# Hourglass attention and quick-GELU MLP: the schedule of batch 0 regrouped over ScalarE, GpSimd and TensorE

## Chip, cores and metric

The kernel runs on one core of a Trainium2 chip. The time is device microseconds of one execution: the median of 3 runs before the change is 320.51 us (320.23, 320.51 and 321.03).

## The reference

Two stages. Stage 1 is attention over q, k, v of 8 batches, 8 heads, 576 positions, head size 64, and is the sum of two parts: a coarse one, on q, k and v averaged over four neighbours (144 positions), repeated four times, and a local one with a band mask of width 3.

```python
q_d = q.reshape(B, H, Sd, factor, D).mean(axis=3)      # factor 4; k_d, v_d alike
out_up = np.repeat(sm_attn(q_d, k_d, v_d), factor, axis=2)
mask = np.abs(pos[:, None] - pos[None, :]) < factor
scores = np.where(mask, scale * np.matmul(q, k.transpose(0, 1, 3, 2)), -1e9)
out_local = np.matmul(softmax(scores), v)
x = (out_up + out_local).transpose(0, 2, 1, 3).reshape(B * S, H * D)
```

Stage 2 is an MLP on the 4608 rows of x (512 wide, hidden 2048):

```python
h = x @ w_in
out = (h * (1.0 / (1.0 + np.exp(-1.702 * h)))) @ w_out
```

## The kernel before, in words

The MLP runs over nine groups of 512 rows. While TensorE works through the MLP of group g, the attention of batch g+1 is woven into it at fixed places (lists POS and POS_0, numbers of MLP steps). Only batch 0 has no MLP beside it: its attention stands in the open at the head of the program, and the change is made there. All engines follow an order written out by hand (a manual schedule): each engine runs its instructions in program order, and waits only for what an instruction needs.

Matrices in PSUM are PA[0], PA[1], PA[2] (two banks each) and PM[0], PM[1] (one bank each). Heads go in four pairs, hp = 0 to 3. For each pair batch 0 does the following:

- **Transposes** (L262, VectorE): k and q of four heads (a quad, qd = 0 or 1) are brought into kT and qT.
- **Sums over four** for the coarse part: `reduce_qk` on VectorE (L281) or `pool_qk` on GpSimd (L292, L296) make kdT and qdT.
- **Scores** on TensorE: local (L360, after a constant bar from L348), coarse (L372). **exp** on ScalarE: L410 and L416.
- **v sums**: `prep_vd_pe`, matmuls with the selection matrix psel (L329) and a copy by ScalarE (L338). psel itself is made of four ramps: GpSimd iotas of 192 and 256 columns (L99, L101), then Abs, Relu and Exp on ScalarE (L170 to L173).
- **AV**: `av_local0` (L519) and `av_down0` (L533, L542) into o[hp], which is PA[0], PA[1], PA[2] and PA[0] again for hp = 0, 1, 2, 3.
- **Normalising**: `normalise0` on VectorE (reciprocal L561, products L564 into yd and L569 into yl), for pairs 0 to 2 in parts "a" and "b".
- **Transposing and summing**: `turned` issues `transp_sum` (L584, L595) on TensorE, and `copy_x` (L607, L611), by which ScalarE writes xT[hp].
- **First MLP product of group 0**: `part`, matmuls of xT[dmc] with w_in (L712), as soon as xT of that pair is there; then Silu on ScalarE (L723), and the second product with w_out (L776).

Ahead of the first `turned` TensorE runs two fp32 matmuls on zeros (`warm(2, t=PM[0], z=wf)`, L657; each appears as two passes), and ScalarE loads the Silu table (L859) and copies the mask (L134). `warm` elsewhere is filler work on bf16 zeros.

GpSimd issues nearly all early loads, in this order: k, q of batch 0 (4 loads), v of batch 0 (10, L216), w_in (4 chunks of 512 columns, L238), k, q of batch 1 (4, L185), w_out 0 and 1 (L247), v of batch 1 chunks 0 to 2 (6 loads), then the GpSimd sums of batch 1, then v chunks 3 and 4 (4 loads), w_out 2 and 3. In the compiled program these loads use eight semaphores in turn: load number n waits on GpSimd until load n-8 has landed. The sums of batch 1's first quad (L292, L296) stand behind the sixth v load of batch 1, which waits for q of batch 1's second quad.

The second product of group 0 has 64 matmuls (numbers 0 to 63): w_out chunk 0 for rows 0 to 255 is used by numbers 0 to 7, chunk 1 by 8 to 15, both for the other rows by 16 to 31, chunk 2 from number 32, chunk 3 from 48. Scores of batch 1 come ahead of number 0 and of number 14, its v sums ahead of number 25, its first AV ahead of number 30.

Of the kernel before, what the change touches and what calls it, by code (L numbers as in the profile page):

```python
# [19 lines left out]
def kernel(  # L20
# [70 lines left out]
    dr = consts.tile([128, 1], FP32, name="dr")  # L91
    bias = consts.tile([128, 4], FP32, name="bias")
    dp = consts.tile([128, 7, 64], FP32, name="dp")
    it = dict(allow_small_or_imprecise_dtypes=True)
    halves = [slice(0, 64), slice(64, 128)]

    def iota_psel():
        for par in range(2):
            nc.gpsimd.iota(dp[halves[par], 0:3], pattern=[[-72, 3], [-8, 64]],  # L99
                           base=2 * (KSTART[par] + 72) - 3, channel_multiplier=2, **it)  # L100
            nc.gpsimd.iota(dp[halves[par], 3:7], pattern=[[72, 2], [-384, 2], [-8, 64]],  # L101
                           base=2 * (KSTART[par] + 114) - 3, channel_multiplier=2, **it)

    def iota_mask():
        for par in range(2):
# [61 lines left out]
        nc.vector.tensor_tensor(out=rv, in0=rv, in1=r2, op=ALU.add)  # L167

    def end_psel():
        nc.scalar.activation(out=dp, in_=dp, func=AF.Abs)  # L170
        nc.scalar.activation(out=dp, in_=dp, func=AF.Relu, bias=bias[:, 3:4])
        for sl, c in ((slice(0, 1), 1), (slice(1, 7), 0)):
            nc.scalar.activation(  # L173
                out=psel[:, sl], in_=dp[:, sl],
                func=AF.Exp, scale=-400.0, bias=bias[:, c : c + 1],
            )
# [17 lines left out]
    def load_qk(b, qd):  # L194
        load_1("k", k, kf, b, qd)
        load_1("q", q, qf, b, qd)
# [40 lines left out]
    def load_w_in(c, n):  # L237
        nc.gpsimd.dma_start(  # L238
            out=w_in_bf[:, :, c : c + n],
            in_=bass.AP(  # L240
                tensor=moe_w_in.tensor, offset=moe_w_in.offset + c,
                ap=[[d_ff, 128], [128 * d_ff, n_dmc], [1, n]],
            ),
        )
# [187 lines left out]
    def banks(t):  # L432
        return t if t is PM else [t[:, u, :] for u in range(2)]

    def av_local(b, hp, o, chunks=range(5)):
        E, vb, o = es[hp], vbs[b % 2], banks(o)
        for i in chunks:
            for par in range(2):
                for j in range(2):
                    pos = j if par == 0 else 1 - j  # L440
                    nc.tensor.matmul(  # L441
                        o[par][64 * pos : 64 * pos + 64, 65 * i : 65 * i + 65],
                        lhsT=E[64 * par : 64 * par + 64, j, 60 * i : 60 * i + 64],
                        rhs=vb[64 * par : 64 * par + 64, i, 2 * hp + j, :],
                        start=True, stop=True,
                        tile_position=(64 * par, 64 * pos),
                    )
# [63 lines left out]
        return x  # L511

    def av_local0(hp, o, chunks):
        E, vb = es[hp], vbs[0]
        for i in chunks:
            for j in range(2):
                for par in range(2):
                    pos, c0 = i % 2, 65 * (i // 2 * 2 + j)
                    nc.tensor.matmul(  # L519
                        o[64 * pos : 64 * pos + 64, par, c0 : c0 + 65],  # L520
                        lhsT=E[64 * par : 64 * par + 64, j, 60 * i : 60 * i + 64],
                        rhs=vb[64 * par : 64 * par + 64, i, 2 * hp + j, :],
                        start=True, stop=True,
                        tile_position=(64 * par, 64 * pos),
                    )

    def av_down0(hp, o):
        Ed, vd, u = eds[hp // 2], vds[0], hp % 2
        h0 = hp - u
        for kc in range(3):  # L530
            for j in range(2):
                q0 = SD * kc + 128
                nc.tensor.matmul(  # L533
                    o[64:128, j, 260:390],
                    lhsT=Ed[64 * j : 64 * j + 48, u, q0 : q0 + 64],
                    rhs=vd[64 * j : 64 * j + 48, kc, h0 : h0 + 2, :],
                    start=(kc == 0), stop=(kc == 2),
                    tile_position=(64 * j, 64),
                )
        for kc in range(3):  # L540
            for j in range(2):
                nc.tensor.matmul(  # L542
                    o[:, j, 390:455],
                    lhsT=Ed[64 * j : 64 * j + 48, u, SD * kc : SD * kc + 128],
                    rhs=vd[64 * j : 64 * j + 48, kc, hp, :],
                    start=(kc == 0), stop=(kc == 2),
                    tile_position=(64 * j, 0),
                )
# [5 lines left out]
            work.tile([128, 2, 7, 1], FP32, name="rc0", tag="rc0", bufs=4),  # L554
        )

    def normalise0(o, y, u, parts="ab"):
        yl, yd, rc = y
        ov = o[:, :, 0:455].rearrange("p x (c e) -> p x c e", e=65)
        c0, c1 = {"a": (0, 4), "b": (4, 7), "ab": (0, 7)}[parts]  # L560
        nc.vector.reciprocal(rc[:, :, c0:c1], ov[:, :, c0:c1, 64:65])  # L561
        if "b" in parts:
            st = 2 - u
            nc.vector.tensor_tensor(  # L564
                out=yd.rearrange("p s x d -> p x s d"), in0=ov[:, :, 4 + u : 7 : st, 0:D],
                in1=rc[:, :, 4 + u : 7 : st].to_broadcast([128, 2, 2, D]), op=ALU.mult,
            )
            c1 = 6
        nc.vector.tensor_tensor(  # L569
            out=yl[:, :, c0:c1], in0=ov[:, :, c0:c1, 0:D],  # L570
            in1=rc[:, :, c0:c1].to_broadcast([128, 2, c1 - c0, D]), op=ALU.mult,
        )
# [247 lines left out]
    fill()  # L820
    for i in range(5):
        load_vb(0, i)
    for c in range(4):
        load_w_in(512 * c, 512)
    for qd in range(NQ):
        load_qk(1, qd)
    load_w_out(0)
    load_w_out(1)
    warm(21, 336)
    make_off()  # L830
    make_ident(di)
# [8 lines left out]
    prep_1("k", 0, 1)  # L840
    prep_1("q", 0, 1)
    reduce_qk(0, 0, "q")
    reduce_qk(0, 1, "k")
    reduce_qk(0, 1, "q")
    warm(10)
    sp = scores(0, 1, PA[0:2])
    exp_local(1, sp)
    exp_down(0, scores_d(0, 0, PA[2]))
    warm(4)
    for hp in range(4):  # L850
        o[hp] = PA[hp % 3]
        y[hp] = y_tiles0()
    prep_vd_pe(0, PM[0], range(0, 2))
    for hp in range(2):
        av_local0(hp, o[hp], range(5))
        normalise0(o[hp], y[hp], hp % 2, "a")
    prep_vd_pe(0, PM[1], range(2, 3))
    exp_down(1, scores_d(0, 1, PA[2]))
    nc.scalar.preload_act_table_set("silu_and_others")  # L859
    for hp in range(2):  # L860
        av_down0(hp, o[hp])
        normalise0(o[hp], y[hp], hp % 2, "b")
    av_local0(2, o[2], range(5))
    normalise0(o[2], y[2], 0, "a")
    warm(2, t=PM[0], z=wf)
    make_mask()

    gT0 = new_gT()
    acc = PM + [PA[n][:, u, :] for n in (1, 2, 0) for u in range(2)]
    late = [acc[n] for n in (0, 1, 6, 2, 4, 0, 1, 7, 0, 1)]  # L870

    def part(ffcs, *dmcs):
        for dmc in dmcs:
# [5 lines left out]
        transp_sum(y[hp], x)  # L879
        copy_x(0, hp, PM if n is None else PA[n][:, :, 0:288])  # L880

    turned(0, None)
    av_down0(2, o[2])
    normalise0(o[2], y[2], 0, "b")
    turned(1, 1)
    av_local0(3, o[3], range(5))
    av_down0(3, o[3])
    normalise0(o[3], y[3], 1)
    part((0, 1), 0)
    turned(2, 2)  # L890
    part((0, 1), 1)
    part((2, 3), 0)
    turned(3, 0)
    part((2, 3), 1)
    part((0, 1, 2, 3), 2)
    part((4, 5), 0, 1, 2)
    part(range(6), 3)
# [4 lines left out]
    for g in range(n_groups):  # L902
        b = g + 1
        if g == 0:
            load_vb(1, 0)
            load_vb(1, 1)
            load_vb(1, 2)
            prep_qk(1, 0)
            pool_qk(1, 0)
            prep_qk(1, 1)  # L910
            load_vb(1, 3)
            load_vb(1, 4)
            load_w_out(2)
            load_w_out(3)
            reduce_qk(1, 1, "q")
            reduce_qk(1, 1, "k")
            for qd in range(NQ):
                load_qk(2, qd)
            nc.gpsimd.memset(v4[32:64], 0.0)
            load_v(2, gate=after(w_out_bf[0:1, 12, 0:1], nc.gpsimd))  # L920
            load_v4(2)
        elif b < B:
            if b > 2:
                load_v4(b)
            prep_qk(b, 0)
            pool_qk(b, 0)
            if b + 1 < B:
                for qd in range(NQ):
                    load_qk(b + 1, qd)
            prep_v(b, nc.gpsimd)  # L930
            if b + 1 < B:
                load_v(b + 1)
            prep_qk(b, 1)
            pool_qk(b, 1)
            prep_v4(b, nc.gpsimd)
        steps = {}
        if b < B:
            for n, f in zip(POS if g else POS_0, attention(b, None if g else (1, 2))):
                steps.setdefault(n, []).append(f)
            if g == 0:  # L940
                steps.setdefault(VDP_0, []).append(lambda: prep_vd_pe(1, flat(PA[2])))
        gT = new_gT() if g else gT0
        mm1(g, gT, steps, 0 if g else 6)
        mm2(g, gT, {n - 16: f for n, f in steps.items() if n >= 16})
# [30 lines left out]
```

## Time and profile before

| What | Value |
|---|---|
| median of 3 runs | 320.51 us |
| profiled execution, first to last instruction | 318.6 us |
| what the median has beyond that span | 1.9 us |
| TensorE busy | 309.5 us (97%) |
| VectorE, ScalarE, GpSimd busy | 133.6, 184.0, 138.9 us |
| mean granted TensorE clock | 1.000 |
| TensorE busy in 0 to 10, 10 to 20, 20 to 30 us | 8.00, 8.55, 9.98 us |
| TensorE busy in 30 to 40, 40 to 50, 50 to 60 us | 9.19, 9.74, 9.58 us |

The time of the profiled execution itself, with what lies around its span, is not listed beside it; the 1.9 us above are the difference between the median of the three runs and the span. In a timeline row the columns are start, duration, engine, line, operation, output and inputs, count, and in brackets how long the engine stood idle ahead of it and who released it. PE is TensorE, PEld its weight loads, DVE is VectorE, ACT is ScalarE, POOL is GpSimd. A busy TensorE is not always at useful work: fillers count as busy.

### The profile page before, as it was taken

To read this page: it belongs to the slowest core of one execution; us is meant where nothing else is said; L and a number is where in the kernel's file an instruction comes from. 1 tells how busy PE (TensorE), PEld (TensorE's weight loads), DVE (VectorE), ACT (ScalarE), POOL (GpSimd) and SP (SyncE) were. 2 spreads that over 40 slices of the span, in tenths; PEclk is the share of its full clock that TensorE was granted. 3 is DMA by queue.
4 is the path that set the end of the run, shared out by engine and by line. 5 is a ranking of instruction groups with operands and counts; after the bars stand their busy time and mean duration, and the time that the engine had idled before them with its cause. 6 is when DMAs were issued, how large, how long until landed. Compare 5 with 4: busy or idle time off the path is not lost.

```text
span 318.6 us, 10993 instructions
## 1 busy us (share of the span) xinstructions
PE 309.5 (97%) x4927; PEld 156.9 (49%) x4927; DVE 133.6 (42%) x222; ACT 184.0 (58%) x314; POOL 138.9 (44%) x168
## 2 busy tenths in 40 slices
PE   7899999999999989999999999999999999999995
PEld 4465455444554545455545554455445544444444
DVE  6963825730684066703780378027811650000000
ACT  4464773577647674658465846674667556415611
POOL 8843782099209930696049703980297000000000
PEclk9999999999999999999999999999999999999999
DMA  7999999999719941598259915991360110020011
GB/s 121 116 191 209 184 90 207 185 270 230 180 39 218 199 114 70 144 216 173 71 134 206 188 41 136 206 205 58 109 107 2 71 68 2 0 99 33 2 65 67
DMA packets 64078, 40.02 MB, mean 126 GB/s; under 512 B 44064, under 2 KB 55456, under 8 KB 64032
## 3 DMA queue, kind: packets, MB, share of 16 engines
q0 software_dynamic: 19392, 14.95, 33.3%
q1 hardware_dynamic: 44496, 24.32, 32.7%
q8 instruction: 38, 0.62, 0.9%
q10 hardware_dynamic: 144, 0.07, 0.1%
q14 instruction: 8, 0.07, 0.1%
HBM read 44.83 MB, written 9.44 MB: 170 GB/s over the span
## 4 chain that ended last, share of the span: by engine, by line
PE 86%; DMA 7%; POOL 4%; issue 1%; ACT 0%; DVE 0%; POOLq 0%
PE pm L776 37%; PE pm L712 33%; DMA kb<-in_k_dram 5%; PE pa L360 3%; PE pa L776 2%; DMA qb<-in_q_dram 2%; PE pa L441 2%; PE pa L712 2%; PE pa L494 2%; PE pa L372 2%; PE pa L463 2%; PE pm L791 1%; POOL w_in_bf L238 1%; POOL vb L216 1%; POOL pq L292 1%
## 5 line engine op out<-in xcount | busy, mean ns | idle before, releaser
L776 PE MATMUL pm<-w_out_bf,gT 128*128 128x512 bf16 x528 | 120.8, 380 | 0.4 <-issue 0.4
L712 PE MATMUL pm<-xT,w_in_bf 128*128 128x512 bf16 x512 | 119.2, 379 | 0.0
L723 ACT ACTIVATE gT<-pm 128x512 bf16<-128x512 f32 x128 | 76.3, 598 | 44.7 <-PE pm L712 44.7
L712 PEld LDWEIGHTS <-w_in_bf 128*128 128x128 bf16 x576 | 55.6, 98 | 66.2
L776 PEld LDWEIGHTS <-gT 128*128 128x128 bf16 x560 | 52.0, 98 | 60.8 <-issue 1.7
L424 DVE TENSOR_TENSOR es<-es,mask 128x600 bf16<-128x600 bf16 x28 | 18.6, 667 | 90.1 <-ACT es L410 89.1
L292 POOL TENSOR_TENSOR pq<-kT 128x576 f32<-128x576 bf16 x13 | 15.1, 1159 | 84.7 <-DVE kT L262 84.7
L761 ACT ACTIVATE osb<-pm 128x512 f32<-128x512 f32 (+2 forms) x35 | 20.5, 586 | 38.3 <-PE pm L776 34.2
L618 ACT COPY od<-pa 128x384 f32<-128x384 f32 (+1 forms) x56 | 19.0, 406 | 26.4 <-PE pa L504 23.3
L480 DVE TENSOR_TENSOR y<-pa,rc 128x896 bf16<-128x896 f32 x28 | 30.6, 1092 | 1.0
L410 ACT ACTIVATE es<-pa 128x600 bf16<-128x600 f32 x32 | 19.7, 668 | 10.8 <-PE pa L360 10.6
L639 DVE TENSOR_TENSOR xT<-pa,od 128x570 bf16<-128x570 f32 x28 | 21.0, 752 | 8.0 <-ACT od L618 8.0
L308 POOL TENSOR_TENSOR v<-v 112x512 f32<-112x512 f32 x18 | 23.9, 1330 | 0.0
L763 DVE TENSOR_SCALAR osb<-pm 128x128 f32<-128x128 f32 x1 | 0.3, 293 | 55.0 <-ACT osb L761 55.0
L262 DVE STREAM_TRANSPOSE kT<-kb 128x576 f32<-128x576 f32 x16 | 20.0, 1248 | 5.6 <-DMA kb<-in_k_dram 5.5
L262 DVE STREAM_TRANSPOSE qT<-qb 128x576 f32<-128x576 f32 x16 | 19.8, 1240 | 0.8 <-DMA qb<-in_q_dram 0.6
L712 PE MATMUL pa<-xT,w_in_bf 128*128 128x512 bf16 x64 | 20.0, 379 | 0.0
L360 PEld LDWEIGHTS <-kT 32*64 32x64 bf16 x1280 | 14.7, 104 | 7.8 <-issue 6.6
L360 PE MATMUL pa<-qT,kT 32*64 32x60 bf16 x1280 | 17.2, 198 | 1.3 <-DVE qT L262 1.3
L216 POOL DMA_DIRECT2D vb<-in_v_dram x20 | 13.7, 699 | 8.1 <-DMA w_in_bf<-in_moe_w_in_dram 3.6
L292 POOL TENSOR_TENSOR pq<-qT 128x576 f32<-128x576 bf16 x13 | 14.9, 1147 | 0.0
L416 ACT ACTIVATE ed<-pa 128x864 bf16<-128x864 f32 x16 | 14.3, 897 | 0.1
(92 smaller groups left out, 278.9 us busy)
## 6 DMA issues: line engine op xcount, KB each, us to landing
out_dram<-osb SPq DMA_DIRECT2D x35, 256.0 KB, 2.1
vf<-in_v_dram SPq DMA_DIRECT2D x60, 128.0 KB, 5.3
v<-in_v_dram SPq DMA_DIRECT2D x36, 192.0 KB, 4.5
kb<-in_k_dram POOLq DMA_DIRECT2D x16, 288.0 KB, 6.5
qb<-in_q_dram POOLq DMA_DIRECT2D x16, 288.0 KB, 7.9
w_in_bf<-in_moe_w_in_dram POOLq DMA_DIRECT2D x4, 512.0 KB, 12.1
w_out_bf<-in_moe_w_out_dram POOLq DMA_DIRECT2D x4, 512.0 KB, 8.7
vb<-in_v_dram POOLq DMA_DIRECT2D x20, 64.0 KB, 5.7
```

Source lines behind the costliest of these rows:

```text
L262: nc.vector.transpose(out=t32.rearrange("p (i c) -> p c i", c=18), in_=store[b, qd].bitcast(FP32).rearrange("p (c d) -> p c d", c=18),)
L292: nc.gpsimd.tensor_tensor(out=t1, in0=sv[:, :, 0:2, :], in1=sv[:, :, 2:4, :], op=ALU.add)
L308: eng.tensor_tensor(out=t1[0:112], in0=x[:, :, 0:2, :], in1=x[:, :, 2:4, :], op=ALU.add)
L360: nc.tensor.matmul(sp[r // 2][64 * par : 64 * par + 64, r % 2, 60 * i : 60 * i + 60], lhsT=kT[b, qd][rows, k0 : k0 + 64, a], rhs=qT[b, qd] ...
L410: nc.scalar.activation(out=es[2 * qd + u][:, :, 0:300], in_=sp[u][:, :, 0:300], func=AF.Exp, scale=inv_sqrt_d,)
L480: nc.vector.tensor_tensor(out=y[:, xs], in0=ov[:, :, :, 0:D], in1=rc[:, xs].to_broadcast([128, n, 7, D]), op=ALU.mult,)
L618: nc.scalar.copy(out=od[:, 4 * t0 : 4 * (t0 + n)].rearrange("p (t f) -> p t f", f=4), in_=x[:, xx, 288 : 288 + n, None].to_broadcast([128, ...
L639: eng.tensor_tensor(out=sub(xT[hp], t0 + 3, (57, 2), (114, 5), (1, 57)), in0=sub(x, 3, (509, 2), (57, 5), (1, 57)), in1=sub(od, 3, (57, 2) ...
L712: nc.tensor.matmul(acc, lhsT=w_in_bf[:, dmc, ffc * 128 : (ffc + 1) * 128], rhs=xT[dmc][:, g * TG : g * TG + TG], start=(dmc == 0), stop=(d ...
L723: nc.scalar.activation(out=gT[:, ffc, :], in_=acc, func=AF.Silu, scale=GELU_SCALE)
L761: eng.activation(out=osb, in_=ap, func=AF.Copy, scale=1.0 / GELU_SCALE)
L776: nc.tensor.matmul(ops[t], lhsT=gT[:, ffc, t * 128 : (t + 1) * 128], rhs=w_out_bf[:, ffc, :], start=(ffc == 0), stop=(ffc == n_ffc - 1),)
```

## The change

- **Ramps.** The four wide iotas become four of 3 and 4 columns (`db`), and seven ScalarE activations of 64 columns (Abs, scale 8, bias from `db`) make the ramps.
- **Second q sum.** The q sum of quad 1 of batch 0 goes from VectorE (`reduce_qk`) to GpSimd (`pool_qk`), ahead of the loads of w_in 1 to 3 and of k, q of batch 1, which are issued behind it; w_in 0 stays ahead of it.
- **Fillers.** The two fp32 filler matmuls are gone; the bf16 fillers stay.
- **Order.** AV of pair 3, then of pair 2 now come ahead of all four `turned`. Pair 3 goes into PM instead of PA[0].
- **Pair 3.** ScalarE copies PM[0] and PM[1] (455 columns each, fp32) into the v4 buffer (`loose`); VectorE takes the reciprocal from there, GpSimd does the two products. The loads of w_out 0 and 1 are issued behind these products.
- **Table and mask.** The Silu table is loaded after the two copies, instead of right after the second coarse exp; the mask is copied between `copy_x` of pair 2 and of pair 3.
- **Targets.** `turned` uses PA[0], PA[1], PA[2], PM; the accumulators of the MLP are renumbered to match.
- **Batch 1.** The v loads of chunk 2 (two loads) go behind GpSimd's sums of quad 0.

```diff
     def iota_psel():
...
-            nc.gpsimd.iota(dp[halves[par], 0:3], pattern=[[-72, 3], [-8, 64]],
-                           base=2 * (KSTART[par] + 72) - 3, channel_multiplier=2, **it)
+            nc.gpsimd.iota(db[sl, 0:3], pattern=[[-72, 3]], base=c + 144,
+                           channel_multiplier=-6, **it)
...
     def end_psel():
-        nc.scalar.activation(out=dp, in_=dp, func=AF.Abs)
+        for m in range(7):
+            nc.scalar.activation(
+                out=dp[:, m], in_=di[:, 0:64], func=AF.Abs, scale=8.0, bias=db[:, m : m + 1]
+            )
...
+    def loose(o):
+        t = v4.rearrange("p k h c -> p (k h c)")[:, 0:910].rearrange("p (x c) -> p x c", x=2)
+        for u in range(2):
+            nc.scalar.copy(out=t[:, u, :], in_=banks(o)[u][:, 0:455])
+        return t
...
-    def normalise0(o, y, u, parts="ab"):
+    def normalise0(o, y, u, parts="ab", eng=nc.vector):
...
     fill()
     for i in range(5):
         load_vb(0, i)
-    for c in range(4):
-        load_w_in(512 * c, 512)
-    for qd in range(NQ):
-        load_qk(1, qd)
-    load_w_out(0)
-    load_w_out(1)
+    load_w_in(0, 512)
...
     reduce_qk(0, 0, "q")
+    pool_qk(0, 1, "q")
     reduce_qk(0, 1, "k")
-    reduce_qk(0, 1, "q")
+    for c in range(1, 4):
+        load_w_in(512 * c, 512)
+    for qd in range(NQ):
+        load_qk(1, qd)
...
-        o[hp] = PA[hp % 3]
+        o[hp] = PA[hp] if hp < 3 else PM
...
     exp_down(1, scores_d(0, 1, PA[2]))
-    nc.scalar.preload_act_table_set("silu_and_others")
     for hp in range(2):
         av_down0(hp, o[hp])
         normalise0(o[hp], y[hp], hp % 2, "b")
-    av_local0(2, o[2], range(5))
-    normalise0(o[2], y[2], 0, "a")
-    warm(2, t=PM[0], z=wf)
-    make_mask()
+    for hp in (3, 2):
+        av_local0(hp, o[hp], range(5))
+        av_down0(hp, o[hp])
+    normalise0(loose(o[3]), y[3], 1, eng=nc.gpsimd)
+    load_w_out(0)
+    load_w_out(1)
+    normalise0(o[2], y[2], 0)
+    nc.scalar.preload_act_table_set("silu_and_others")
...
-    turned(0, None)
-    av_down0(2, o[2])
-    normalise0(o[2], y[2], 0, "b")
+    turned(0, 0)
     turned(1, 1)
-    av_local0(3, o[3], range(5))
-    av_down0(3, o[3])
-    normalise0(o[3], y[3], 1)
     part((0, 1), 0)
-    turned(2, 2)
     part((0, 1), 1)
     part((2, 3), 0)
-    turned(3, 0)
+    turned(2, 2)
+    make_mask()
     part((2, 3), 1)
+    turned(3, None)
     part((0, 1, 2, 3), 2)
...
             load_vb(1, 0)
             load_vb(1, 1)
-            load_vb(1, 2)
             prep_qk(1, 0)
             pool_qk(1, 0)
             prep_qk(1, 1)
+            load_vb(1, 2)
```

## Prediction

> **What bounds the kernel now.** I read the page's engine shares and the chain of waits first, then TensorE's idle time by stretches of 10 us, then the timeline from 15 to 52 us row by row. Times are us from the span's start.
>
> ```profile
> PE 309.5 (97%) x4927; PEld 156.9 (49%) x4927; DVE 133.6 (42%) x222; ACT 184.0 (58%) x314; POOL 138.9 (44%) x168
> ...
> PE 86%; DMA 7%; POOL 4%; issue 1%; ACT 0%; DVE 0%; POOLq 0%
> ```
>
> TensorE sets the end: 97% busy, 86% of the chain. What isn't TensorE in the chain (DMA 7%, GpSimd 4%) lies ahead of 40 us; behind that the chain is matmuls. So time can be had only where TensorE idles or runs fillers in the first 60 us, and what is won there is kept if no later wait takes it. The timeline shows the two places, and who is late next:
>
> ```profile
> 18.69 1.28 ACT L859 ACT_TABLE_LOAD   x1
> ...
> 19.42 2.16 PE L657 MATMUL pm<-wf 128*128 128x512 f32 x4
> ...
> 22.02 0.70 ACT L607 CAST xT<-pm 128x288 bf16<-128x288 f32 x2 [1.35 <-PE pm L595]
> ...
> 23.80 0.60 PE L712 MATMUL pm<-xT,w_in_bf 128*128 128x512 bf16 x2
> ...
> 35.40 0.68 POOL L216 DMA_DIRECT2D vb<-in_v_dram  x1 [0.72 <-DMA qb<-in_q_dram]
> 36.14 1.15 POOL L292 TENSOR_TENSOR pq<-kT 128x576 f32<-128x576 bf16 x1
> ...
> 39.22 0.67 POOL L296 TENSOR_TENSOR qdT<-pq 128x288 bf16<-128x288 f32 x1
> ...
> 39.94 0.26 PE L372 MATMUL pa<-qdT,kdT 32*64 32x144 bf16 x4 [0.81 <-POOL qdT L296]
> ...
> 41.30 2.04 POOL L216 DMA_DIRECT2D vb<-in_v_dram  x3 [0.77 <-DMA w_out_bf<-in_moe_w_out_dram]
> 43.31 1.54 POOL L247 DMA_DIRECT2D w_out_bf<-in_moe_w_out_dram  x2
> ...
> 51.05 1.03 PE L776 MATMUL pm<-w_out_bf,gT 128*128 128x512 bf16 x4
> ```
>
> First place: the fp32 fillers, 2.16 us of TensorE, then the transposes from 21.42, then the MLP from 23.80. Second: at 39.94 TensorE has waited 0.81 us for GpSimd's sum, which began at 36.14 only because GpSimd stood in front of a v load until 35.40. Next in line are transfers: w_out 1 ends GpSimd's wait at 41.30 (landed 41.02) and is used at 42.4; w_out 2, issued at 43.31, landed at 50.27 and is used at 51.05, a slack of 0.78.
>
> **The change part by part.** *Ramps.* Four iotas (4.42 to 5.72) become four tiny ones (nearest rows: 0.14 for 128x1, 0.20 for 64x60), so the first seven v loads go out some 0.7 earlier. The eighth waited for q's landing (GpSimd released at 11.39), so it, the two behind it and w_in 0 at 13.40 stay. ScalarE gets seven 64-column activations (row 128x64: 0.35) for one of 0.58: 4.95 + 2.45 + 0.67 + 0.86 = 8.9, ahead of the first exp at 9.19; that gap hides it, and beyond it another 0.6 (TensorE's bar waits for the exps, done at 10.42, and comes at 11.03). I take 0; bounds 0 to 0.5 gain, because TensorE waits 0.4 and 0.3 for v at 15.05 and 15.98.
>
> *Second q sum.* VectorE loses 1.34 (14.69 to 16.03); it then idled 0.76 anyhow: 0. GpSimd does it behind w_in 0: 14.2 + 1.15 + 0.67 + gaps = 16.1, used at 17.15. The new wait (for qT, ready at 12.38) is over by then. Queued behind are three w_in and four q, k loads, 1.9 later. Their issues go to 16.1 and on; w_in 0 took 1.55 from issue to its first packet, so w_in 1 can flow from 17.65, and the first of the sixteen shares of w_in 0 landed at 18.4, the last at 21.95: hidden by 0.75, and all later landings follow in order of issue as before. If that cover went, they would move by the excess.
>
> *Fillers and order.* TensorE from 19.11: AV of pair 3 0.31 + 0.48, AV of pair 2 the same (rows L519, L533, L542), to 20.7; transposes of pairs 0 and 1 (0.55 to 0.6 each) to 21.85. ScalarE: second coarse exp ends at 18.67; waits for pair 3 till 19.95; two copies of 455 columns. No such row: between 0.40 (288 columns) and 0.59 (512 columns); by the slope of 256 to 512 (0.38, 0.59) 0.54, two overlapped as the row of two (0.70 for 2 x 0.40) 0.97; to 20.95. The table load, hidden before, now comes behind: 1.28, to 22.23. Copy of x 0: 0.64, to 22.87; of x 1 to 23.45. So the MLP starts at 22.9 instead of 23.80, TensorE idling 1.05 where the fillers were worth 2.16.
>
> From there: two matmuls 0.43, a wait of 0.1 for x 1, four matmuls, transposes 2, two matmuls, transposes 3 at 25.3, ten matmuls to 28.0, where the last six of the first accumulators begin (28.77 before). **Gain 0.77** at the MLP's first product, which is dense to its end (38.79, now 38.0); w_in 1 (landed 24.45) is needed at 26.7, w_in 2 (26.96) at 31. The mask (0.69) is behind x 2 and ahead of x 3, 26.8, needed at 28.0: hidden.
>
> *Pair 3 on GpSimd.* The reciprocal waits for ScalarE's copies; behind it on VectorE stands pair 2's normalising, ready by 22.9 for 24.3: 0. GpSimd's products start at 21.3. No row: below, VectorE's 0.42 + 0.95; above, GpSimd's slowest fp32 sum (1.505 for 512 columns) times 2 for 1024 columns, 3.0. I take its median, 1.268 x 2 = 2.5, ready at 23.85, needed at 25.3: hidden by 1.4. Behind them stand w_out 0 and 1, issued at 24 and 25 (22.23 and 24.74 before); their packets begin at 33: 0.
>
> *Batch 1's sums.* They now wait for the fourth v load (32.64 + 0.68) instead of the sixth: 33.4 + 3.75 (36.14 to 39.89) = 37.1, needed at 38.1. **The 0.81 goes.** Two v loads go behind, 37.1 to 38.4; the queue reaches v of batch 1 at 37.5 and has four loads first: 0.
>
> **Sum.** Scores of batch 1 begin at 38.0 and take 1.08 without the wait (38.79 to 40.68 less 0.81), so number 0 of the second product goes from 40.68 to 39.1, 1.58 ahead. Next late: w_out 1, used by number 8 at 40.83, landed 41.02: 0.23 back, 1.36 kept. Batch 1's v is needed at 46.3, landed 46.20: 0. Number 32 comes at 49.7. w_out 2 waits on GpSimd for the same landings, so is issued at 43.31 again; in the trace fifteen of its sixteen shares had landed by 49.59, the last at 50.27. That last one coincides with an instruction fetch (one 16 KB packet of 0.94 us at 49.17 in the DMA view), which goes with the program's progress and would come 1.3 earlier, on any engine; only the last four shares (49.29 to 49.59) have no 0.7 to spare. So bounds 0.73 (50.27 + 0.05) and 1.36 (49.59); I take 49.8, nearer to the fifteen: **gain 1.2**. Behind 52 us the slack is larger (w_out 3 landed 52.81, used 55.4). The profiled span goes from 318.6 to 317.4; with the 1.9 that the median has beyond the span, 319.3.
>
> **Rivals.**
> *w_out 2 as late as before* (a wait in place of the removed ones): 51.05 - 50.32 = 0.73, 319.8. For it: the slack of 0.78 is in the trace. It is also where we land if the early part brings nothing, since the 0.81 alone reaches this cap: the change then doesn't do what it says.
> *GpSimd's products at twice the row*: 5.1, ready at 26.4, transposes 3 late by 1.1; 1.58 - 1.1 = 0.5, 320.0. Decides from 4.0 us on. Against it: all 18 rows lie within 1.262 and 1.505.
> *The clock drops without fillers* (slower). The first 21 fillers, of 336 columns, take 5.79, 0.27 each, where ten of 512 columns take 2.33 at 9.07: TensorE begins slow, and rises after some 5.4 us of work. Afterwards its longest idle is 0.81, and the granted clock stays 1.00. The new gap of 1.05, behind small tiles only, is longer than any that the trace shows harmless. If it costs another 5.4 us at half speed: 2.7 lost, 0.77 - 2.7 + 0.81 = -1.1, 321.6. It decides from an idle between 0.81 and 1.05 on.
> *More*: v earlier (0.3) and w_out 1 without its straggler (fifteen shares at 39.49, the last at 41.02): 1.58 + 0.3 = 1.9, 318.6.
>
> The Trainium skill (TensorE: Matmul & The Clock Gate, Part 1) has the clock fall only after an idle window of about 3.4 us; by that rule the clock rival would not come, and its chance would go to the forecast. The trace does not contradict it, but has no gap over 0.81 to try it on, so the rival keeps its chance.
>
> **How the numbers follow.** Forecast 0.44 (319.3); w_out 2 late or the early part void 0.26 (319.8); GpSimd slow 0.07 (320.0); clock 0.15 (321.6); more 0.08 (318.6). 0.3% is 0.96 us, about what a measurement of this kernel can tell from no change: faster 0.52, same 0.33, slower 0.15. The range runs from 318.5 to 320.9: it takes in all but the clock case, with some 0.4 above 320.0 and the spread of the runs (0.8).
>
> **What would show it.** Right: the MLP's first matmul near 22.9, transposes 3 near 25.3 without a wait for GpSimd, GpSimd's last sum for batch 1 near 37.1, no wait of TensorE for it, number 32 near 49.8 with a short DMA wait. Wrong: matmuls of 512 columns at over 0.4 us from start to start after 22 (clock); GpSimd's products over 4 us; w_in 1 landing after 25; or a wait behind 52 us that eats the gain.

## The result, and the profile after

The changed kernel took 322.23 us (median of 20 executions, 320.17 to 323.85), the kernel before 320.90 beside it (20 executions, 319.32 to 322.43): ratio 1.0038, 95% interval 1.0020 to 1.0056. It is slower, and outside the range. The ratios below leave out three executions that ran longer than the rest: one of e9, the profiled one of e13 (356.16 us, at a granted clock of 0.85 throughout), and one of the kernel before beside e13 and e14.

The page of the kernel after: TensorE's busy line, the granted clock in 40 slices of 8 us, and the shares of the chain of waits.

```profile
PE 303.3 (94%) x4872; PEld 157.4 (49%) x4923; DVE 129.4 (40%) x217; ACT 185.8 (58%) x322; POOL 141.9 (44%) x172
...
PEclk9987999999999999999999999999999999999999
...
PE 91%; issue 4%; DMA 2%; DVE 1%; POOL 1%; ACT 1%; POOLq 0%
```

The profiled execution is the slowest of the 20 (323.85 us). The clock dips in the third and fourth slice. "Issue", in which TensorE waits for nothing that the profile shows, has 4% of the chain, against 1% in the profile before, and DMA and GpSimd together 3%, against 11%. Neither share is due to the change alone: the kernel before, unchanged, has nearly the same shares in its second profile (e17 below):

```profile
PE 92%; issue 3%; DVE 2%; DMA 2%; ACT 0%; POOL 0%; POOLq 0%
```

The lower busy time of TensorE is no sign either, since 51 of its matmuls have no record (4872 stand beside 4923 weight loads). So the loss is read from the timeline. The timeline of the kernel after (start, duration, engine, line, operation, and in brackets the idle time ahead of it with its releaser) has the places where TensorE stands; its line numbers are 9 to 11 above those of before:

```profile
15.38 0.81 PE L668 MATMUL pm<-wz 128*128 128x512 bf16 x3 [1.45 <-issue]
...
21.77 0.43 PE L544 MATMUL pm<-vd,ed 48*64 48x130 bf16 x4 [1.76 <-issue]
...
22.50 0.98 ACT L443 COPY v<-pm 128x455 f32<-128x455 f32 x2 [3.33 <-PE pm L553]
...
23.50 1.28 ACT L879 ACT_TABLE_LOAD   x1
...
23.84 0.61 POOL L575 TENSOR_TENSOR yd<-v,rc 128x256 bf16<-128x256 f32 x1 [3.54 <-DVE rc L572]
...
24.42 1.47 POOL L580 TENSOR_TENSOR yl<-v,rc 128x768 bf16<-128x768 f32 x1
...
25.48 0.59 PE L723 MATMUL pa<-xT,w_in_bf 128*128 128x512 bf16 x1
...
35.34 0.66 POOL L301 TENSOR_TENSOR qdT<-pq 128x288 bf16<-128x288 f32 x1
...
42.93 3.20 PE L787 MATMUL pm<-w_out_bf,gT 128*128 128x512 bf16 x13
```

TensorE stands ahead of the first of four bf16 fillers, and 1.76 us in the middle of pair 3's coarse AV, where neither operands nor buffers change. (The first filler's matmul is one of those without a record. The next filler's weight load, which in the other profiles starts with it, is at 15.16, so the first stall is 1.23 us and not the 1.45 of the row. e7 and e8 lack the same record, and their first stalls below are counted alike.) Everything behind the second stall is late by it: ScalarE's two copies of pair 3, the table load, x 0, and so the MLP's first product at 25.48 (predicted 22.9). The second product starts at 42.93 (predicted 39.1). The same table by stretches shows the clock (columns: stretch, its length, busy time and count of TensorE, weight loads, VectorE, ScalarE, GpSimd, then the granted clock, DMA share, GB/s):

```profile
18.30:21.70 3.40, 1.43 (x46) 1.04 (x46) 2.46 (x8) 0.88 (x1) 2.00 (x4) 1.00 1.22 196
21.70:25.10 3.40, 3.33 (x60) 2.53 (x61) 1.55 (x4) 2.57 (x4) 1.25 (x2) 0.50 1.24 207
25.10:28.50 3.40, 3.18 (x17) 1.60 (x16) 0.08 (x1) 0.97 (x2) 3.01 (x4) 0.50 1.20 214
28.50:32.00 3.50, 3.50 (x34) 2.06 (x33) 1.96 (x2) 1.83 (x4) 1.80 (x3) 1.00 1.10 208
```

For 6.83 us the clock is at one half, two steps of 3.41. Matmuls of 512 columns start 0.43 us apart in the third row (26.29, 26.72, 27.14, 27.57) and 0.22 apart in the fourth (29.76, 29.98, 30.19).

From 22.9 to 25.48 goes like this: AV of pair 3 starts 0.51 late (19.62 against 19.11), the second stall is 1.76, and the rest of that AV takes 0.28 longer at half clock; sum 2.55 of 2.58. To 42.93 it is 3.83 behind the prediction. The first MLP product and its transposes took 16.46 (25.48 to 41.94) where I had 15.1; these 1.36 fit the products at half clock up to 28.53.

### The profile page after: what moved, and what is told of

It reads as the page before. It is cut to its first block, busy times and chain, and to the rows that moved or that the text cites. A ratio compares the mean times of both kernels' runs of the same rounds, so it can differ in the third digit from the quotient of the medians.

```text
span 322.0 us, 10941 instructions
## 1 busy us (share of the span) xinstructions
PE 303.3 (94%) x4872; PEld 157.4 (49%) x4923; DVE 129.4 (40%) x217; ACT 185.8 (58%) x322; POOL 141.9 (44%) x172
## 4 chain that ended last, share of the span: by engine, by line
PE 91%; issue 4%; DMA 2%; DVE 1%; POOL 1%; ACT 1%; POOLq 0%
PE pm L787 35%; PE pm L723 34%; PE pa L723 5%; PE pa L365 3%; PE pa L787 2%; DMA qb<-in_q_dram 2%; PE pa L452 2%; PE pa L377 2%; PE pa L505 2%; PE pa L474 2%; PE pm L802 1%; PE pa L595 0%; PE pa L606 0%; PE pa L515 0%; DVE qT L267 0%
## 5 line engine op out<-in xcount | busy, mean ns | idle before, releaser
L787 PE MATMUL pm<-w_out_bf,gT 128*128 128x512 bf16 x499 | 114.4, 380 | 4.2 <-issue 4.1
L723 PE MATMUL pm<-xT,w_in_bf 128*128 128x512 bf16 x488 | 116.0, 380 | 0.8
L734 ACT ACTIVATE gT<-pm 128x512 bf16<-128x512 f32 x126 | 75.2, 598 | 42.7 <-PE pm L723 42.7
L429 DVE TENSOR_TENSOR es<-es,mask 128x600 bf16<-128x600 bf16 x28 | 17.8, 636 | 94.7 <-ACT es L415 93.5
L297 POOL TENSOR_TENSOR pq<-kT 128x576 f32<-128x576 bf16 x13 | 15.1, 1161 | 89.2 <-DVE kT L267 89.2
L723 PE MATMUL pa<-xT,w_in_bf 128*128 128x512 bf16 x71 | 22.6, 397 | 0.2 <-ACT xT L622 0.2
L297 POOL TENSOR_TENSOR pq<-qT 128x576 f32<-128x576 bf16 x14 | 16.0, 1145 | 0.1
(97 smaller groups left out, 278.0 us busy)
```

The source lines that it names most:

```text
L297: nc.gpsimd.tensor_tensor(out=t1, in0=sv[:, :, 0:2, :], in1=sv[:, :, 2:4, :], op=ALU.add)
L723: nc.tensor.matmul(acc, lhsT=w_in_bf[:, dmc, ffc * 128 : (ffc + 1) * 128], rhs=xT[dmc][:, g * TG : g * TG + TG], start=(dmc == 0), stop=(d ...
L734: nc.scalar.activation(out=gT[:, ffc, :], in_=acc, func=AF.Silu, scale=GELU_SCALE)
L787: nc.tensor.matmul(ops[t], lhsT=gT[:, ffc, t * 128 : (t + 1) * 128], rhs=w_out_bf[:, ffc, :], start=(ffc == 0), stop=(ffc == n_ffc - 1),)
```

## The experiments

My theory (*fetch*) was that TensorE takes its instructions in blocks and outran them: in e1, whose profile lacks no record there, the two stalls lie 128 matmuls and 128 weight loads apart, 256 instructions, and the page counts 38 packets of 16 KB in TensorE's instruction queue for some 9,850 instructions, one packet per 256. The rival (*clock alone*) was that the fillers held the clock and nothing else matters. Executions in which the clock fell are told from the others by their mean granted clock: 0.995 is one step of 3.41 us at half speed, 0.989 two, and "held" below means 0.998 or more. The kernel before held it in 129 of 136 executions, the changed one in 9 of 20.

**e1, the changed kernel once more** (no edit).

> The changed kernel once more, unchanged, for a second profile. Theory F (instruction fetch): TensorE stands twice for instructions that have not arrived, at the same two places of the program as in the first profile (behind the first of the four bf16 fillers, 1.45 us at 13.9, and behind the second coarse AV matmul of pair 3, 1.76 us at 20.0), each within 0.5 us of that size; whether the granted clock falls to 0.5 afterwards depends on where its window lies. Rival C (clock alone): the clock falls again near 21.7 us, and the two idle stretches need not come back at those instructions.

321.91 us. The stalls came at the same two places:

```profile
14.88 1.02 PE L668 MATMUL pm<-wz 128*128 128x512 bf16 x4 [1.03 <-issue]
...
22.03 0.30 PE L544 MATMUL pm<-vd,ed 48*64 48x130 bf16 x4 [2.31 <-issue]
```

The second is 0.55 longer than in the first profile, a little more than the 0.5 that I had allowed. So the stalls belong to the program, not to one execution.

**e2, wide ramps back.** `iota_psel` and `end_psel` as before; the rest of the change stays.

> The changed kernel with the ramps of before (wide iotas, one Abs), so the v loads are issued some 0.7 us later again. Theory F: the 16 KB instruction packet that came at 12.0 us comes near 11 as before, the first stall (1.45 us) falls below 0.4, the second stays over 1 us; time 0.3 to 1.0 us below the change, ratio to before 1.000 to 1.003. Rival (ramps are free): both stalls stay, ratio 1.004 as for the change.

1.0034 (1.0006 to 1.0063). The first stall shrank to 0.42, the second is there (1.43 at 20.64); clock held in 3 of 12. The ramps bring the first stall, not the second. The time hardly followed: 321.90 us against 322.23 for the change, and a ratio just above the 1.000 to 1.003 that I expected.

**e3, the fp32 fillers ahead of pair 3's AV.**

```diff
+    warm(2, t=PM[0], z=wf)
     for hp in (3, 2):
         av_local0(hp, o[hp], range(5))
```

> The changed kernel with the two fp32 fillers put back, ahead of the AV of pair 3: 2.16 us of work in few instructions. Theory F: the next block of instructions arrives under them, so the stall in the AV of pair 3 falls from 1.76 to under 0.4 us, the clock stays at 1.00, the MLP's first matmul comes near 25 as in the change but at full speed: 1.5 us less than the profile of the change, ratio to before 0.998 to 1.001. Rival C (the fillers only hold the clock): the clock stays too, but the stall stays at 1.8 us behind the fillers, and the ratio is 1.003 or more.

1.0039 (1.0008 to 1.0069). The second stall is gone and the clock held in 10 of 12, yet the time did not fall:

```profile
20.16 1.98 PE L668 MATMUL pm<-wf 128*128 128x512 f32 x4
...
25.79 0.38 PE L723 MATMUL pa<-xT,w_in_bf 128*128 128x512 bf16 x1 [1.21 <-ACT xT L622]
```

The fillers cost what the stall cost, and here all of it is on the path. Clock alone is thus not the cause. The 1.21 us gap ahead of the MLP cost no clock.

**e4, the kernel before without fp32 fillers.** `warm(2, t=PM[0], z=wf)` taken out.

> The kernel before without its two fp32 fillers, nothing else. Theory F: the transposes of pair 0 would be ready at 19.5 us but their instructions stand behind the same block border, so TensorE idles 1 us or more for issue ahead of or in the transposes of pair 0, and gains less than 1 us; ratio 0.997 to 1.000 if the clock stays, up to 1.004 if it falls. Rival C: no such stall, the clock falls for several us, ratio 1.003 or more. Third possibility, fillers are pure loss: transposes at 19.6, ratio 0.995.

1.0004 (0.9982 to 1.0026); clock held in 5 of 12. The block border now gives a stall here too:

```profile
20.00 0.19 PE L584 MATMUL pm<-id,yd 128*128 128x64 bf16 x1 [0.54 <-issue]
```

The fillers did two jobs, time for the block and the clock; without them the saved TensorE time is given back.

**e5, the third v load of batch 1 alone.** In the kernel before, `load_vb(1, 2)` moved behind `prep_qk(1, 1)`.

> The kernel before with one part of the change alone: the third v load of batch 1 is issued behind GpSimd's sums for batch 1 and not ahead of them. My sum: TensorE's wait of 0.81 us ahead of batch 1's coarse scores goes, w_out 2 lands about 50.3 and takes some 0.05 back, so about 0.75 us less, ratio 0.9977. Fetch theory: nothing in the first 30 us changes, so no stall and no clock drop, and the 0.75 shows in the median. Rival (this part brings nothing, since another wait takes its place): ratio 1.000.

1.0007 (0.9981 to 1.0033). The wait for GpSimd is gone, the gain is not there; e16 to e18 tell why.

**e6, the block border shifted.** The same filler columns in more instructions: `warm(21, 336)` to `warm(38, 186)`, `warm(10)` to `warm(20, 256)`, `warm(4)` to `warm(8, 256)`.

> The changed kernel with its 35 bf16 fillers split into 66 shorter ones of about the same total columns, so that 62 more TensorE instructions stand ahead of the AV of batch 0. Fetch theory (TensorE waits for its next block of 256 instructions): the second stall, 254 instructions behind the first, moves with the count: from the coarse AV of pair 3 some 62 instructions earlier in the program, to the coarse AV of pairs 0 and 1 or the first products of pair 3; the first one moves out of the bf16 fillers into the scores ahead of them. Rival (the stall belongs to pair 3's AV, by its buffers or by a semaphore that the profile doesn't show): it stays in the coarse AV of pair 3. Time within 1 us of the changed kernel by both, 321 to 323.5.

1.0051 (1.0024 to 1.0078), clock held in 1 of 10. The first stall moved by the count, out of the fillers into the scores ahead of them, between the 77th and the 78th of 80 equal matmuls:

```profile
11.88 0.81 PE L365 MATMUL pa<-qT,kT 32*64 32x60 bf16 x77
14.65 0.26 PE L365 MATMUL pa<-qT,kT 32*64 32x60 bf16 x3 [1.95 <-issue]
```

The stall of pair 3's AV vanished, as it is not at a border now; but none came in its place, which I had expected: the block between has 5.7 us of work here (14.65 to 20.37), enough for the packet (17.64 to 18.59). The time did not fall with that stall. No semaphore and no buffer could move with a count.

**e7, loads and second q sum as before.** `reduce_qk(0, 1, "q")` on VectorE, w_in 1 to 3 and batch 1's q, k loads ahead of the sums.

> The changed kernel with the second q sum on VectorE again and w_in 1 to 3 and batch 1's q and k loads issued ahead of the sums as before (w_out 0 and 1 stay late). Fetch theory in its form that the instruction packets queue behind data transfers: with the loads earlier the traffic at 12 to 19 us is as dense, so both stalls stay within 0.5 us of theirs (1.0 to 1.5 and 1.4 to 2.3) and the time is 321.5 to 322.5. Rival (the moved loads delay the packets): the stalls fall under 0.7 together, first w_in product at 23.5 or sooner, time about 320.

1.0061 (1.0024 to 1.0097), stalls 1.42 and 1.27, clock held in 0 of 6; the median, 323.11 us, is above the 322.5 that I expected at most. Moving the sum and these loads didn't bring the loss.

**e8, the early parts alone.** The kernel before with the ramps, the q sum on GpSimd and the loads behind it.

> The kernel before with the early parts of the change alone: ramps on ScalarE, second q sum on GpSimd, w_in 1 to 3, batch 1's q, k and w_out 0, 1 issued behind it; order of TensorE, fp32 fillers and table load as before. My sum had these two parts at nothing: ratio 1.000, first w_in product at 23.8. Fetch theory: the ramps bring the first stall (1.0 to 1.5 us at about 13.9, as with the ramps in the changed kernel), 0.5 us of it reaches the AV; the fp32 fillers give time for the next block, so no second stall, and the clock stays at 1.0; ratio 1.000 to 1.002. Rival (early parts carry the loss): first w_in product at 25 or later, ratio 1.004.

1.0035 (1.0004 to 1.0067), clock held in 10 of 10, first stall 1.48, first product at 24.82 instead of 23.80. Each theory was half right: the stall, the held clock and the absent second stall are those of the fetch theory, but the early parts cost more than I gave them.

**e9, fillers of a sixteenth of the array.** After eight profiles of variants I had a second theory: the clock goes by the share of the array that works in a step of 3.41 us, not by idle time.

```diff
-    warm(2, t=PM[0], z=wf)
+    for _ in range(2):
+        nc.tensor.matmul(
+            PM[0][0:32, 0:512], lhsT=wf[0:32, 0:32], rhs=wf[0:32, 0:512],
+            start=True, stop=True,
+        )
```

> The kernel before with its two fp32 fillers of 128 x 128 made 32 x 32: the same instructions, the same 512 columns, the same 2.16 us, but a sixteenth of the array. Array theory (the clock of the next window of 3.41 us falls when the share of the array that worked in the window is under some 30%; in the ten profiles so far the windows before a drop have 11 to 30% and the others 29% or more): in the profile the window around 18 to 22 us comes to some 20 to 30%, and the mean granted clock is 0.995 or less in at least 5 of 12 runs, as without fillers (7 of 12), against 4 of 60 for the kernel before. Rival (idle time decides, and TensorE is as busy as before): 0.998 or more in at least 10 of 12. Time: about that of the kernel before plus 1 us in the runs with a drop.

1.0032 (1.0000 to 1.0063); clock held in 2 of 12. TensorE was busy throughout, with no stall:

```profile
18.71 2.00 PE L866 MATMUL pm<-wf 32*32 32x512 f32 x4
```

The stretches of that profile, the step before the drop first:

```profile
17.00:20.40 3.40, 3.06 (x52) 1.39 (x48) 3.26 (x11) 2.87 (x3) 1.73 (x3) 1.00 1.23 200
20.40:23.80 3.40, 3.40 (x51) 2.48 (x54) 1.04 (x4) 0.80 (x3) 0.75 (x1) 0.50 1.24 207
```

TensorE was busy 3.06 of 3.40 us, and the clock fell all the same. Its work in that step, columns streamed times rows and columns of the array used, comes to 13% of what dense 128x128 matmuls do (I had expected 20 to 30%). The idle-time rival falls.

**e10, no bulk loads beside the AV.** In the changed kernel w_in 0 to 3 and batch 1's q, k loads stand behind pair 3's products on GpSimd.

> The changed kernel with w_in 0 to 3 and batch 1's q and k loads issued only behind pair 3's products on GpSimd, so that beside batch 0's v nothing is loaded until some 24 us. Theory that the instruction packets wait behind data: the second packet starts within 2 us of TensorE's passing the first border (4.0 in the changed kernel), the second stall falls under 0.7 us; the first one, which has v's loads beside it, stays over 0.8. Rival (the packet is slow by itself): starts 4 us behind, second stall 1.4 or more. The MLP has to wait for w_in, so the time is no measure here (w_in 0 not before 27).

330.71 us, since the MLP waits for w_in, as expected. The row of stretches over the block that ended in the second stall, e10 first, then the changed kernel (DMA share and GB/s are the last two columns):

```profile
15.10:20.00 4.90, 4.51 (x132) 2.88 (x131) 2.61 (x8) 2.03 (x4) 0.00 (x0) 1.00 0.04 5
```

```profile
15.40:20.00 4.60, 4.26 (x127) 2.70 (x126) 2.59 (x8) 1.85 (x3) 4.60 (x8) 1.00 1.12 161
```

With 5 GB/s beside it the packet starts 1.1 us after the border, with 161 GB/s 4.3 us after; the second stall is gone (under 0.05), the first (1.22) stays. This is one execution, but in none of the others, with the loads beside it, does that packet start sooner than 1.8 us after its border. That fits a packet that waits behind data.

**e11, the ramps alone** in the kernel before.

> The kernel before with the ramps on ScalarE alone. Fetch theory: v's first seven loads go out 0.7 sooner, the instruction packet that is asked for at 9.1 starts at 11.5 to 12.9 (10.6 to 11.2 without the ramps in four profiles), TensorE stands 0.8 to 1.7 us at the first border, at 13 to 14 us; no second stall, clock 1.0; ratio 1.001 to 1.004. Rival (the moved sum and loads cost what the early parts cost): no stall, ratio 1.000.

1.0024 (1.0002 to 1.0045), clock held in 10 of 12:

```profile
14.62 1.02 PE L662 MATMUL pm<-wz 128*128 128x512 bf16 x4 [0.90 <-issue]
...
21.64 1.02 PE L662 MATMUL pm<-wf 128*128 128x512 f32 x2 [1.13 <-issue]
```

A second stall came as well, against my expectation, between the fp32 fillers.

**e12 and e15, two edits of the kernel before**, the v load of e5 and `warm(1, t=PM[0], z=wf)`, on two chips.

> A candidate that beats both: the kernel before with the third v load of batch 1 behind GpSimd's sums and one fp32 filler in place of two. By my reading the one filler (1.08 us) still lies across the block border and keeps the array share over 30%, the MLP starts 0.4 sooner, the 0.81 goes: 1.1 us less, ratio 0.9965, clock held in 10 of 12 runs. Rival (the first 40 us are not kept to the end): ratio 1.000.

> The kernel of e12 once more (third v load behind GpSimd's sums, one fp32 filler). If its gain is the kernel's own: ratio 0.994 to 0.998 again. If it was chance of that session: 0.998 to 1.001, as the sum of its parts.

e12: 0.9952 (0.9926 to 0.9978). e15: 1.0002 (0.9982 to 1.0022). The gain did not come again; in e15's profile both borders stall (0.89 and 0.58), in e12's neither. A version that beats the kernel before was not found.

**e13, one fp32 filler instead of two; e14, the change cured**: wide ramps, and `warm(1, t=PM[0], z=wf)` ahead of pair 3's AV.

> The kernel before with one fp32 filler in place of two. If both edits of e12 bring their share: the MLP starts 0.4 to 0.6 sooner (23.3), the wait of 0.81 for GpSimd's sums stays, ratio 0.9985 (0.5 us), clock held. Rival (the filler carries all of e12's gain): ratio 0.9955. Rival (the v load carries it): 1.000.

> The changed kernel with the wide ramps of before and one fp32 filler (1.08 us, whole array) ahead of pair 3's AV. Fetch and array theories together: no first stall; of the second (1.43 without the filler) some 0.4 is left; the window around 19 us rises from 30 to over 45% of the array and the clock is held in at least 9 of 12 runs (3 of 12 without the filler); first w_in product at about 24.2, since the filler lies where the stall was; time 1 to 1.5 us under the changed kernel with wide ramps (321.9): ratio 0.999 to 1.000. Rival (the order itself costs the time): ratio 1.003, clock held or not.

e13: 1.0009 (0.9985 to 1.0032), nothing. e14: 1.0041 (1.0020 to 1.0062), clock held in 11 of 12. The timeline of e14:

```profile
18.85 1.12 PE L664 MATMUL pm<-wf 128*128 128x512 f32 x2
...
20.64 0.36 PE L540 MATMUL pm<-vd,ed 48*64 48x130 bf16 x6 [0.35 <-issue]
...
24.21 1.56 PE L719 MATMUL pa<-xT,w_in_bf 128*128 128x512 bf16 x6 [1.21 <-ACT xT L618]
```

The second stall, the clock and the first product are as expected; a first stall of 0.40, which I had not expected, is there too. The time is not as expected: it is as slow as the changed kernel. 24.21 is 0.4 to 0.7 later than the kernel before (23.50 to 23.80 in three profiles), since with AV ahead of the transposes the filler delays ScalarE's copies, the table load and x 0, one behind the other. That is about half of the 1.3 us in the ratio (0.0041 x 320); the rest I can't place. The profiled execution doesn't show it: it took 319.49 us, less than the median of the kernel before beside it (320.02).

**e16, the v load again; e17 and e18, the kernel before twice more.**

> The kernel of e5 once more (third v load behind GpSimd's sums, two fillers), beside e15. By my sum of the wait (0.75 us) 0.9977; by e5's run 1.0007; e15 should be 0.3 to 0.5 us faster than this one if the filler's 1.08 us counts for as much as the first product's start showed (23.43 against 22.43).

> The kernel before, unchanged, for a second profile. If the wait is a property of the kernel: TensorE waits 0.7 to 0.9 us for GpSimd's sum again, with the MLP's first product at 23.8 and the second product's at 40.7. If it only takes up what came late before it (an instruction block): where the first product starts later than 23.8 by x, the wait is 0.81 less x, and the second product still starts at 40.7 to 40.9.

> The kernel before, unchanged, for a third profile; as for the second.

e16: 1.0006 (0.9980 to 1.0033); e15 was not faster beside it (320.17 us against 320.00). e17 and e18 took 319.78 and 321.30 us. The timeline of e17 around the second product's attention:

```profile
33.81 0.68 POOL L216 DMA_DIRECT2D vb<-in_v_dram  x1 [0.72 <-DMA qb<-in_q_dram]
...
37.63 0.67 POOL L296 TENSOR_TENSOR qdT<-pq 128x288 bf16<-128x288 f32 x1
...
38.72 0.27 PE L372 MATMUL pa<-qdT,kdT 32*64 32x144 bf16 x4
```

Batch 1's q landed 1.6 us sooner than in the first profile, GpSimd's sum ended at 38.30, and there is no wait; nor in e18 (37.96, scores at 39.00), nor in e4. Their second products start at 39.47 and 39.75, not 40.68. Neither of my two readings holds: the wait is no property of the kernel, and it doesn't take up earlier delays either; it depends on when q lands.

## Why the prediction was wrong, point by point

**Ramps** (0, bounds 0 to 0.5 gain): wrong. Alone they cost 0.0024 of 320, 0.8 us (0.1 to 1.4); taken out of the change they gave back little (e2: 1.0034 of 1.0038). Their own sums held (seven activations 1.78 us, hidden). What I had as a possible gain, v's loads going out sooner, is the likely cause: the packet that follows TensorE's passing of the border at about 9.1 us started at 11.45 to 12.90 in the eight profiles with the ramps, and at 10.54 to 11.98 (middle 11.05) in the eleven others that I compared; the stall at the next border is 0.90 to 1.95 in the first, 0 to 0.89 in the others. The two groups touch. That v's loads in particular do it was not tried by themselves; e10 has it for the bulk loads, in one execution.

**Second q sum** (0): w_in 1 went out at 15.88, as worked out (16.1), and nothing waited for it (the first share of w_in 0 had landed at 18.71 in the profile before, not at 18.4, so its cover was larger than I had it); e7 shows that undoing it gains nothing.

**Fillers and order** (MLP at 22.9, gain 0.77): this is the step that failed. The chain to 22.9 was right in its links: copies 0.98 (predicted 0.97), the gap of TensorE 1.21 in e3, e6 and e14 (predicted 1.05). But I took the fillers for TensorE time and nothing else, and TensorE's instructions for always there. The one instruction packet that I had looked at, at 49.17, I had counted as a hindrance to the load of w_out 2 only. The fillers also kept TensorE from reaching the next border of its instructions too soon. With pair 3's and pair 2's AV pulled together, 256 small instructions pass in 4.8 us (15.16 to 20.0), and the packet needs longer. The MLP's first product came at 25.48 instead of 22.9, 1.7 later than before instead of 0.9 sooner. The passing of a border, the packet and the restart (us), from the records of single packets and matmuls in the traces:

| profile | border passed | packet | next border reached | goes on |
|---|---|---|---|---|
| before | 14.09 | 16.25 to 19.06 | 20.54 | 20.56 |
| after | 15.16 | 19.42 to 20.38 | 20.00 | 21.77 |
| e1 | 14.88 | 19.58 to 20.53 | 19.72 | 22.03 |
| e2 | 14.07 | 18.33 to 19.28 | 19.20 | 20.64 |
| e4 | 13.80 | 16.94 to 18.72 | 19.46 | 20.00 |
| e10 | 15.14 | 16.25 to 17.18 | 20.05 | at once |

Wherever TensorE stalls at one of these two borders, in any profile, it goes on 1.3 to 1.8 us after its packet's end; the kernel before reaches the border 1.5 behind that end, with nothing to spare. The Trainium skill (Runtime: NRT & Kernel Launch, Instruction fetch mechanics) describes a first-in, first-out instruction memory for each engine, refilled in 16 KiB blocks of 256 instructions by the sequencer's own DMA queue, and calls its cost "mostly hidden". The size agrees with the 38 packets; that the cost is hidden does not hold here, with stalls of 0.4 to 2.3 us (161 GB/s of data in the row of the kernel after).

**The clock rival** (slower, 321.6, chance 0.15) came, but not from the gap that I gave it: gaps of 1.21 us cost no clock in e3, e6 and e14. I worked out the array's share in every step of 3.41 us from the rise of the clock to 45 us, in all profiles that have full clock, each matmul spread over its duration and an fp32 pass counted like a bf16 one: under 25% the clock fell each time (6 steps), at 31% or more never, between (26 to 30%) three times of ten. Counted by where a matmul starts, the bounds shift by some points, so the numbers are rough. In the kernel after the deciding step had 12%. In the changed kernel's 20 executions those that held the clock average 321.64 (9), the others 322.50 (11); all 20 average 322.11, those of the kernel before 320.88. So of the 1.2 between the averages about 0.5 (0.86 in 11 of 20) comes with the clock, and the 0.8 that is left without it. No edit that took a stall and the loss of the clock away brought the time back (e3: 1.0039, e14: 1.0041), since its filler stood on the path in the stall's place. That the stalls make up these 0.8 is therefore argued from the profiles, not shown. The rule that I weighed against the rival (TensorE: Matmul & The Clock Gate, Part 1 of the Trainium skill, an idle window of 3.4 us) has the length of the step right: the stretches in the traces are 3.41, 6.83 and 17.07. As to what counts as idle, the measurement decides: 3.06 us of matmuls in 3.40 were not enough in e9.

**Pair 3 on GpSimd** (2.5, hidden): right; 0.61 + 1.47 = 2.08, ready at 25.89, used by the transposes at 29.23.

**Batch 1's sums** (0.81 goes): right that the edit takes the wait away (GpSimd's last sum 36.0, predicted 37.1), wrong that it was there to be won. It stood in one profile, and not in e4, e17, e18; e5 and e16 bring no gain. So the *sum* (gain 1.2) lost both of its terms, and the cap by w_out 2 was never reached. The rival for an early part that brings nothing ("the change then doesn't do what it says") stood at 319.8, since it too counted on this 0.81.

**Open**: some 0.6 us of e14, and why e12 and e15 differ by 0.5%.

**The spread behind 45 us** has the same source. In the 19 profiles other than e13's TensorE waits 32 more times for "issue" behind 45 us for 0.4 us or longer, up to 1.56. All 32 waits lie within 4 weight loads of a border (a multiple of 128 loads from the first one), and all 32 end 1.2 to 1.7 us after the end of a 16 KB instruction packet. Many stand near 58, 88, 119 and 217 us, in each profile a different choice of them (e2, e5 and e14 have none). Leaving out e10 too, the waits for "issue" behind the start of the second product come to 0.3 to 3.0 us a profile, and without them the rest takes 276.5 to 278.0 us. So chance alone moves an execution by as much as the effects that the experiments look for.

## What to carry to other kernels

Ahead of pulling small matmuls together, count TensorE's instructions: here TensorE stood 0.35 us or more at the second border in 9 of 19 profiles, behind blocks of 256 instructions with 4.8 to 6.2 us of work. The length alone doesn't decide: 5.8 us in e9 and 4.9 in e10 brought no stall, because the packet came early. Fillers that look idle may be what covers it. A filler is worth its share of the array as well as its time, so replace it only by work that fills the array. And a wait that is to be won should be seen in more than one execution: the 0.81 us was in one of four profiles.

## What the runs showed of the hardware that I had not expected

The granted clock fell with TensorE busy 90% of the step, on 32x32 matmuls (e9), and the way up may have a threshold of its own: at half clock the steps with 33, 34 and 35% of the array stayed there, those from 36% on rose. That margin is no wider than the way of counting. An instruction packet that takes 0.9 us or more to move started 1.1 us after its border without data traffic and 1.8 to 4.7 with it, and the stall that it causes shows in the profile as "issue".
